# Making the second part of the first chunk's in-place sum four gate steps earlier, and part of another sum one step earlier

## The chip, the cores and the metric

The kernel runs on one core of one Trainium2 chip. The metric is the device time of one execution in microseconds (us). "PE" is TensorE (matmuls), "PEld" its weight loads, "DVE" VectorE, "ACT" ScalarE, "POOL" GpSimd, "SP" the engine that issues most transfers.

## The reference, cut to what matters

```python
xn = _layernorm(x)                               # x: 2048 rows of 448
s  = attention(xn @ wq, k_cache, v_cache) @ wo   # 16 heads of 256, window of 512 keys
g  = silu((gelu(xn @ w_gate) * (xn @ w_up)) @ w_down)    # F = 1792
return x + s * g
```

Only `g` for the first 512 rows (the first *chunk*) concerns the change. The kernel takes the rows in four chunks of 512, and F in 14 tiles of 128.

## The kernel before

The kernel keeps its own list of operations and of buffers. An operation that writes a buffer waits for the buffer's last writer and readers, and one that reads it waits for its writer:

```python
    def op(self, eng, fn, reads=(), writes=(), dma=False, after=()):
        o = Op(eng, fn, dma)
        raw = {b.writer: None for b in reads if b.writer is not None}
        deps = dict(raw)
        for b in writes:
            if b.writer is not None:
                deps[b.writer] = None
            deps.update((x, None) for x in b.readers)
        ...
```

A gate step makes two tiles of `gelu(gate) * up`. ACT applies the gelu, DVE multiplies and writes the tile `actTh` (512 columns, one buffer `b_actT[chunk][tile]`):

```python
        def gu_evac(n, b):
            c, f = divmod(n, NF)
            s = n % NGL
            act(gl[:, s, :], bank[b], ACT.Gelu_apprx_tanh, (b_ps[b],), (b_gl[s],))
            K.op("dve", lambda e: e.tensor_tensor(actTh[:, c % 2, f, :], bank[b + 1], gl[:, s, :], ALU.mult),
                 (b_ps[b + 1], b_gl[s]), (b_actT[c % 2][f],))
```

The down projection of a chunk uses seven products in place of eight (a Strassen-like scheme). For that, DVE first forms four sums of activation halves (`k` = 0 to 3), each in two parts (`i` = 0: four tiles, `i` = 1: three tiles). Sum `k = 0` goes *in place*: left half minus right half of tiles 0 to 6, written over the right half.

```python
        dn[0][0][3] = (actTh[:, 0, 0:NH, HC:QC], b_actT[0][0:NH])
        ...
            j, (x, bx), (y, by), op = ((3, o(0, 0), o(0, 1), ALU.subtract), (2, o(1, 1), S(3), ALU.subtract),
                                       (0, S(2), o(0, 0), ALU.add), (1, o(1, 0), S(2), ALU.subtract))[k]
            add("dve", S(j)[0], x, y, bx + by, S(j)[1], op)
        ...
        def down7(c, banks, g, b_g, order=(3, 6, 5, 4, 2, 1), then=None):
            ...
            product(0, B1, A(0, 0))              # "product one": left halves of tiles 0 to 6
            ...
            what = {3: (B4, A(1, 1)), 6: (B7, S(3)), 5: (B6, S(2)), 4: (B5, S(0)), 2: (B3, S(1)), 1: (B1, A(1, 0))}
            for j in order:                      # "product two" to "product seven"
                product(j, *what[j], j != 1)
```

The loop over gate steps queues these sums, from lists of (step, sum). `n` is even, and tiles `n` and `n + 1` are made in one step; the first chunk is `n` = 0 to 13, the second 14 to 27. The first chunk's down projection follows step 26.

```python
        for n in range(4, NU, 2):
            gu_group((n, n + 1), cur)
            gu_evac(n, cur[0])
            ...
            while WD_SUMS and n >= WD_SUMS[0][0]:
                sum_wd(*WD_SUMS.pop(0)[1])
            while ACT_SUMS and n >= ACT_SUMS[0][0]:
                sum_act(*ACT_SUMS.pop(0)[1])
            ...
            if n + 1 in DOWN_AT:
                ...
                end = down7(DOWN_AT[n + 1], ...)
```

The softmax here doesn't subtract the row's maximum and nothing guards it: scores larger than these inputs give would overflow.

## Time and profile before

| what | value |
|---|---|
| median, first three runs | 542.15 us |
| span of the profiled execution (541.71 us) | 539.9 us |
| PE busy | 532.9 us, 99% |
| DVE busy | 383.8 us, 71% |
| waits of PE for a sum of activations | one, 0.6 us, ending at 50.62 us |

How to read it: `bank` is a tile that matmuls write, and an *evacuation* is the operation that reads a bank out into another tile. `wdh` and `wdt` are the down weights, cast to 16 bits, and sums of them; `sd` holds the sums `k` = 1 to 3. In the attention, `kT` is keys, `va` values, `pn` softmax weights and `pT` their transpose. The prediction below shows the lines of the page, of the waits of PE, of the chain that ended last and of the timelines of PE and DVE around 50 us. In a timeline line the columns are start, length, engine, source line, operation, output and inputs, shape and count. A bracket gives the idle time before and what ended it.

### The profile page before, as it was taken

The page shows a single profiled execution, that of the slowest core. Times are in us where ns is not written, and L with a number is a line of the kernel's source. Part 1 is how long each engine was busy: PE and PEld are TensorE (multiplying, and loading weights), DVE is VectorE, ACT ScalarE, POOL GpSimd, SP SyncE. Part 2 cuts the span into 40 slices and gives each one's busy share as a digit, 9 for nine tenths or more (in the row PEclk, how much of TensorE's full clock was granted, in tenths as well). Part 3 has the DMA queues.
Part 4 walks back from the last instruction along what each step waited for, and adds up shares of the span by engine and source line. Part 5 has one row for each costly group of instructions (what it writes and reads, how often), then busy time and mean ns, then how long its engine had stood idle before and what let it go on. Part 6 is the DMA issues. An engine that isn't in the chain of part 4 may idle for free.

```text
span 539.9 us, 10920 instructions
## 1 busy us (share of the span) xinstructions
PE 532.9 (99%) x4155; PEld 310.9 (58%) x4180; DVE 383.8 (71%) x839; ACT 314.0 (58%) x782; POOL 40.1 (7%) x78
## 2 busy tenths in 40 slices
PE   9999999999999999999999999999999999999998
PEld 5556657449644444984444469544444984444487
DVE  6689785799767757935875786366667934776785
ACT  5466354873668768116866850488488106876820
POOL 1131120000000010003001000120000003001010
PEclk9999999999999999999999999999999999999999
DMA  9569172942596776302861860067448302772821
GB/s 295 125 186 108 55 124 76 263 101 46 114 186 137 154 186 153 60 1 83 167 141 50 152 137 1 18 156 140 95 106 147 70 1 69 164 158 73 148 66 35
DMA packets 171604, 61.38 MB, mean 114 GB/s; under 512 B 155104, under 2 KB 168416, under 8 KB 171552
## 3 DMA queue, kind: packets, MB, share of 16 engines
q1 hardware_dynamic: 167488, 51.30, 44.5%
q0 software_dynamic: 3008, 8.72, 6.7%
q8 instruction: 33, 0.54, 0.4%
q10 hardware_dynamic: 1056, 0.66, 0.4%
q14 instruction: 19, 0.16, 0.1%
HBM read 19.76 MB, written 3.67 MB: 43 GB/s over the span
## 4 chain that ended last, share of the span: by engine, by line
PE 92%; DVE 2%; ACT 2%; DMA 2%; issue 1%; ACTq 0%
PE bank L394 91%; ACT p L830 2%; DMA pT<-pn 2%; DVE pn L837 1%; PE bank L511 1%; DVE actTh L560 0%; DVE rden L834 0%; DVE wdt L388 0%; PE bank L492 0%; ACT gl L385 0%; DVE actTh L388 0%; DVE sd L388 0%; ACT oTh L385 0%; DVE xnT L884 0%; DVE gl L424 0%
## 5 line engine op out<-in xcount | busy, mean ns | idle before, releaser
L830 ACT ACTIVATE p<-bank 128x512 f32<-128x512 f32 x256 | 150.4, 596 | 28.1 <-DVE pn L837 25.9
L394 PE MATMUL bank<-pT,va 128*128 128x512 bf16 x512 | 120.8, 379 | 0.3
L394 PE MATMUL bank<-kT,qT 128*128 128x512 bf16 x487 | 117.8, 379 | 2.3 <-ACT qT L385 1.0
L837 DVE TENSOR_SCALAR pn<-p,rden 128x512 bf16<-128x512 f32 x256 | 113.0, 484 | 9.1 <-DMA pT<-pn 4.8
L394 PE MATMUL bank<-xnT,wq 64*128 64x512 bf16 x768 | 94.9, 376 | 0.0
L394 PEld LDWEIGHTS bank<-pT,va 128*128 128x128 bf16 x512 | 49.6, 98 | 61.3 <-DMA pT<-pn 2.3
L394 PEld LDWEIGHTS bank<-kT,qT 128*128 128x128 bf16 x512 | 49.3, 98 | 61.7 <-issue 3.4
L394 PE MATMUL bank<-xnT,wgu 64*128 64x512 bf16 (+2 forms) x768 | 84.0, 350 | 0.1
L385 ACT ACTIVATE qT<-bank 128x512 bf16<-128x512 f32 x76 | 44.1, 596 | 51.6 <-PE bank L394 49.9
L815 DVE CAST qT<-bank 128x512 bf16<-128x512 f32 x52 | 34.8, 690 | 49.3 <-PE bank L394 49.3
L394 PEld LDWEIGHTS bank<-xnT,wq 64*128 64x128 bf16 x768 | 36.7, 94 | 46.3 <-ACT p L830 1.7
L394 PEld LDWEIGHTS bank<-xnT,wgu 64*128 64x128 bf16 x768 | 37.7, 94 | 35.8 <-issue 0.6
L834 DVE RECIPROCAL rden<-rsum 128x2 f32<-128x2 f32 x128 | 21.2, 166 | 46.7 <-ACT p L830 46.5
L830 ACT ACTIVATION_READ_ACCUMULATOR p<-bank 128x1 f32 x256 | 51.6, 201 | 0.0
L394 PE MATMUL bank<-wt,sr 128*128 128x224 f16 x512 | 50.0, 259 | 0.0
L394 PEld LDWEIGHTS bank<-wt,sr 128*128 128x128 f16 x512 | 49.0, 98 | 0.4 <-ACT oTh L385 0.2
L385 ACT ACTIVATE gl<-bank 128x512 bf16<-128x512 f32 x56 | 33.0, 596 | 26.4 <-PE bank L394 22.1
L560 DVE TENSOR_TENSOR actTh<-bank,gl 128x512 f16<-128x512 f32 x56 | 37.4, 688 | 11.9 <-PE bank L394 6.4
L855 DVE TENSOR_SCALAR oTh<-bank 128x512 f16<-128x512 f32 x62 | 42.4, 684 | 0.0
L385 ACT ACTIVATE oTh<-bank 128x512 f16<-128x512 f32 x66 | 38.9, 589 | 3.9 <-PE bank L394 3.9
L394 PE MATMUL bank<-wt,oTh 128*128 128x224 f16 (+1 forms) x416 | 38.4, 252 | 0.0
L394 PEld LDWEIGHTS bank<-wt,oTh 128*128 128x128 f16 x416 | 37.2, 98 | 0.9
(77 smaller groups left out, 387.9 us busy)
## 6 DMA issues: line engine op xcount, KB each, us to landing
wtb<-in_A_wo_dram POOLq DMA_DIRECT2D x4, 896.0 KB, 10.5
wq<-in_A_wq_dram SPq DMA_DIRECT2D x2, 1536.0 KB, 8.5
va<-in_A_v_cache_dram SPq DMA_DIRECT2D x8, 256.0 KB, 6.2
pT<-pn SPq DMA_TRANSPOSE x128, 2.8
xr<-in_A_x_dram POOLq DMA_DIRECT2D x15, 112.0 KB, 2.3
wd<-in_B_w_down_dram SPq DMA_DIRECT2D x1, 1568.0 KB, 8.0
g<-g_all POOLq DMA_DIRECT2D x14, 112.0 KB, 2.3
out_dram<-xr POOLq DMA_DIRECT2D x12, 112.0 KB, 2.1
```

The source lines that it names most:

```text
L385: K.op("act", lambda e, o=o, i=i: e.activation(o, i, func, scale=scale), reads, writes)
L394: ins = e.matmul(o, lhsT=l, rhs=r, start=st, stop=sp, skip_group_check=True)
L511: ins = e.matmul(bank[b][:, 0:w], lhsT=gl[:, 0, 0:P], rhs=gl[:, 0, 0:w], start=True, stop=True)
L560: K.op("dve", lambda e: e.tensor_tensor(actTh[:, c % 2, f, :], bank[b + 1], gl[:, s, :], ALU.mult), (b_ps[b + 1], b_gl[s]), (b_actT[c % 2] ...
L815: K.op("dve", lambda v, s=s, b=b: v.tensor_copy(qT[:, s, 1, :], bank[b + 1]), (b_ps[b + 1],), (b_qT[s][1],))
L830: K.op("act", lambda e, b=b, r=r, z=z: e.activation(p32[:, z, :], bank[b], ACT.Exp, scale=att_scale, accum_out=rsum[:, r:r + 1]), (b_ps[b] ...
L834: K.op("dve", lambda e, r=r: e.reciprocal(rden[:, r - 1:r + 1], rsum[:, r - 1:r + 1]), b_rsum[r - 1:r + 1], b_rden[r - 1:r + 1])
L837: K.op("dve", lambda e, r=r - 1 + t, z=(n - 1 + t) % NP32, y=y, t=t: e.tensor_scalar(pn[:, y, t, :], p32[:, z, :], rden[:, r:r + 1], None, ...
L855: K.op("dve", lambda v, i=i, b=b: v.tensor_scalar(oTh[:, i, :], bank[b], WS, None, op0=ALU.mult), (b_ps[b],), (b_oT[i],))
```

## The change

The intent is to take the second part of the in-place sum away from the end of the second chunk's gate steps, where it stands just ahead of the down projection, and to make it at step `n = 16`. Counted in pairs of tiles from 0 over both chunks that is pair number 8, thus the second pair of the second chunk. Before, the sum was queued for 23, reached at `n = 24`.

```diff
-        ACT_SUMS = [(n, (c, k, i)) for c, i, ns in ((0, 0, (10, 11, 19, 21)), (0, 1, (23, 23, 25, 25)),
+        ACT_SUMS = sorted([(n, (c, k, i)) for c, i, ns in ((0, 0, (10, 10, 20, 22)), (0, 1, (16, 24, 26, 26)),
                                                     (1, 0, (30, 32, 34, 34)), (1, 1, (36, 36, 38, 38)))
-                    for k, n in enumerate(ns)]
+                    for k, n in enumerate(ns)], key=lambda x: x[0])
```

Since `n` is even, 11 means 12, 19 means 20, and so on. Two sums therefore move: the in-place sum's second part from 24 to 16, and the first part of the second sum (`k = 1`, tiles 7 to 10) from 12 to 10. The sorting is needed because the list is popped from its front.

## The prediction

> **What bounds the kernel now.** I began with the page. Its first part and the shares of its chain say that TensorE sets the time almost everywhere:
>
> ```profile
> PE 532.9 (99%) x4155; PEld 310.9 (58%) x4180; DVE 383.8 (71%) x839; ACT 314.0 (58%) x782; POOL 40.1 (7%) x78
> ...
> PE 92%; DVE 2%; ACT 2%; DMA 2%; issue 1%; ACTq 0%
> ```
>
> PE is counted busy for 532.9 of 539.9 us, and 92% of the chain that ended last is PE work. So the changed sums, which are VectorE work, count only where PE waits for VectorE. The waits of PE over the whole span are four lines:
>
> ```profile
> PE bank L511 <- DVE epst L425: 1.2, 1, 1.2
> PE bank L394 <- ACT qT L385: 1.0, 6, 0.2
> PE bank L394 <- DVE actTh L388: 0.6, 1, 0.6
> PE bank L394 <- issue: 0.5, 3, 0.2
> ```
>
> The third is one wait of 0.6 us for a sum over the activations (L388 is the helper for all such sums). The chain in order of time shows where: it is PE from 9.76 to about 44 us, leaves PE through VectorE, and returns at 50.62 us:
>
> ```profile
> 47.93 1.28 DVE actTh L560 x2
> 49.21 0.88 DVE wdt L388
> 50.09 0.48 DVE actTh L388
> 50.57 0.05 issue
> 50.62 67.62 PE bank L394 x644
> ```
>
> The last VectorE piece ahead of PE's return is the in-place sum, 50.09 to 50.57 us. The timeline of PE there is:
>
> ```profile
> 48.52 1.48 PE L394 MATMUL bank<-xnT,wgu 64*128 64x512 bf16 x12
> 50.62 1.52 PE L394 MATMUL bank<-wdh,actTh 128*128 128x224 f16 x14 [0.63 <-DVE actTh L388]
> 51.97 2.85 PE L394 MATMUL bank<-wdt,actTh 128*128 128x224 f16 x28
> ```
>
> That is the end of the second chunk's gate matmuls and the start of the first chunk's down projection (seven products of 14 matmuls). Its first product reads the left halves of the first chunk's activations. The in-place sum writes the right halves of the same tiles, and the kernel tracks a tile as one buffer, so the product waits for a sum whose result it doesn't read. The down projection of the second chunk has the same shape and no such wait, and gives the undisturbed rhythm:
>
> ```profile
> 76.96 1.46 PE L394 MATMUL bank<-xnT,wgu 64*128 64x512 bf16 x12
> 78.35 1.52 PE L394 MATMUL bank<-wdh,actTh 128*128 128x224 f16 x14
> 79.71 2.85 PE L394 MATMUL bank<-wdt,actTh 128*128 128x224 f16 x28
> ```
>
> **What the Trainium skill says.** "Perfetto Trace Analysis", section Tensor Engine Instruction, says that a matmul's recorded end is estimated and not observed. So I measure the stall from start to start, not by the 0.63 us idle that the timeline prints: undisturbed, product one starts 78.35 - 76.96 = 1.39 us after the last 12 gate matmuls start; here it takes 50.62 - 48.52 = 2.10 us. The stall is 0.71 us. The trace agrees with the page in that recorded matmuls overlap their successors (76.96 + 1.46 is after 78.35). "TensorE: Matmul & The Clock Gate", Part 3, section The mechanism, says matmuls start and end in strict program order; so product two can't slip past a blocked product one. The trace agrees: product two starts 1.35 us after product one, though its own operand was finished at 50.09. "VectorE: DVE Perf Modes", section Side-by-side (where the cycles go), gives 16-bit two-source operations two elements a cycle at 0.96 GHz, 0.52 ns an element. This trace agrees: the sums of 768 elements last 0.55 us and those of 1792 last 1.09 us, so 0.54 us / 1024 = 0.53 ns an element and about 0.15 us fixed. A move therefore changes no sum's duration by itself.
>
> **The change part by part.** The sums are issued after the gate steps, which run in twos. Comparing the instruction orders of the two kernels, PE, ACT, POOL and SP keep theirs; on VectorE two instructions move, and none is added or dropped.
>
> *Moved one:* the in-place sum over tiles 4 to 6 of the first chunk (768 elements, 0.55 us) goes from 50.01 us, behind the last sum over the down weights, to behind the statistics at 37.34 us. In the timeline of VectorE, with the idle before and its releaser in brackets:
>
> ```profile
> 36.69 0.62 DVE L441 BATCH_NORM_STATS2 stats<-x 128x6 f32<-128x448 bf16 x1
> 37.34 0.18 DVE L444 BATCH_NORM_AGGREGATE mv<-stats 128x2 f32<-128x6 f32 x1
> 37.99 0.69 DVE L560 TENSOR_TENSOR actTh<-bank,gl 128x512 f16<-128x512 f32 x1 [0.47 <-PE bank L394]
> ```
>
> VectorE sits idle there for 37.99 - (37.34 + 0.18) = 0.47 us. A sum that follows such an aggregate starts 0.10 us after the aggregate's start (the one at 30.93, after 30.83), so this one runs from about 37.44 to 37.99, and back-to-back records overlap by 0.08 us (52.27 + 0.55 against 52.74). The evacuation at 37.99 is then late by 0 to 0.05 us, and 0.31 us of idle at 38.99, a wait for POOL, absorbs more. Cost at its new place: 0.
>
> *Moved two:* the second sum over tiles 7 to 10 (1024 elements, 0.66 us) goes forward one step, from 30.93 us to the end of the first in-place sum at 27.54 + 0.68 = 28.22. The idle there is 0.71 us, up to 28.93, so it fits with 0.05 us to spare at most. PE uses those banks again only about 3 us after this; cost 0, gain 0.
>
> *What PE gains:* product one no longer waits for that sum. In the changed kernel its wait is on ACT (a cast of down weights, over at 44.54 + 1.74 = 46.28 us, and the last reader of its bank, over by 47.66), so nothing holds it at 48.52 + 1.39 = 49.91 us. Gain 50.62 - 49.91 = 0.71 us. The VectorE wait moves to product two, which needs the last weight sum. That ends at 50.09 as before, and product two starts at 49.91 + 1.35 = 51.26, so 1.17 us in hand. Product four needs the second sum over tiles 11 to 13, which slides forward to about 50.01 and ends at 50.57; PE reaches it at 54.66 - 0.71 = 53.95. Product five is reached at 55.3, and the sums left after the two evacuations end about 0.5 us earlier than the 53.29 of before. Nothing new binds.
>
> *Sum:* PE is 0.71 us earlier from 50 us on. The rest to the end is started by PE or bound by it, so the shift should be carried through: 542.15 - 0.71 = 541.44, rounded to 541.45. Busy time of VectorE stays at 383.8 us.
>
> **The rivals.** *A: the wait is replaced.* Product two would wait for the weight sum instead, and part of 0.71 us come back. For it: VectorE is nearly unbroken from 43.16 to 53.2 us (10.01 us busy of 10.04), and the chain runs through it. Against: the 1.17 us in hand, since product one itself takes 1.35 us. If VectorE were late by 1.5 us, the gain would shrink to 0.4 us: 541.8. *B: the gain is given back later.* The chain leaves PE again between 371 and 419 us for the softmax (activation p, pn and the transposes to pT). For it: a fixed-time arrival there would swallow the 0.7 us and give 542.1. Against: these chains start from PE's own scores, so they shift with it, and none of PE's four waits is for a DMA; PEld's waits for pT total 2.3 us in five places, so small realignments of a few tenths are possible either way. *C: the new places hurt.* If the sum at 37.4 us pushed an evacuation so far that PE waited for a bank in a later gate step, the loss could be some tenths: 541.8 to 542.3. Against: 0.47 and 0.71 us of idle under sums that take 0.55 and 0.66, and VectorE's wait for PE and POOL resets the lateness before the backlog begins. *D: more than the stall.* VectorE is earlier by 0.5 us through the epilogue of the down projection, but PE has no other wait there, so nothing adds to 0.71; only run spread could give 540.9.
>
> **Range and chances.** The centre is 541.45. The three runs of before span 542.05 to 542.58, 0.5 us, nearly the size of the effect. Allowing 0.4 us below (favourable realignment) and 0.5 us above (part of A, B or C, or spread) gives 541.0 to 542.0. The expected change is 0.71 / 542.15 = 0.13%, far inside 2%, which would take 10.8 us: within 2% 0.99, faster 0.005, slower 0.005.
>
> **What would show each step right or wrong.** Right: the waits of PE lose their line for actTh at L388; product one starts 1.39 us after the start of the last 12 gate matmuls, near 49.9 us, with product two 1.35 us later; the chain stays on PE through 44 to 50 us; the moved sums stand at about 37.4 and 28.3 us, with the idle after them gone; total VectorE busy is unchanged. Wrong: a wait of PE for wdt (A), a PE wait for an evacuation at L560 near 41 to 49 us (C), or starts that are 0.7 us earlier at 60 us but not at 400 us (B). A time at or above 542.1, outside run spread, would make the prediction wrong, and so would one below 540.9.

## The result, and the profile after

The changed kernel took 541.78 us (median of 6 runs, 541.28 to 541.98), beside 542.21 us for the kernel before (6 runs, 541.93 to 542.61). The ratio is 0.9989, with a 95% interval of 0.9977 to 1.0002. All ratios here are not quite the ratio of the medians, nor always that of the plain means. The time is inside the predicted range.

The timeline of PE in the profile after, at the same place as in the prediction's lines:

```profile
48.51 1.48 PE L394 MATMUL bank<-xnT,wgu 64*128 64x512 bf16 x12
49.91 1.51 PE L394 MATMUL bank<-wdh,actTh 128*128 128x224 f16 x14
51.27 2.85 PE L394 MATMUL bank<-wdt,actTh 128*128 128x224 f16 x28
```

Product one starts at 49.91 us, 1.40 us after the last 12 gate matmuls, and has no idle bracket any more. Before, it was 50.62 us. Product two starts 1.36 us later, without a wait. The chain of the profile after, in order of time (start, length, what), no longer leaves PE between 44 and 50 us:

```profile
9.75 107.78 PE bank L394 x1056
117.53 0.18 issue
117.72 11.07 PE bank L394 x105
```

The timeline of DVE shows where the two sums went:

```profile
28.24 0.69 DVE L388 TENSOR_TENSOR sd<-actTh 128x1024 f16<-128x1024 f16 x1
28.92 1.34 DVE L560 TENSOR_TENSOR actTh<-bank,gl 128x512 f16<-128x512 f32 x2
...
37.33 0.18 DVE L444 BATCH_NORM_AGGREGATE mv<-stats 128x2 f32<-128x6 f32 x1
37.43 0.52 DVE L388 TENSOR_TENSOR actTh<-actTh 128x768 f16<-128x768 f16 x1
37.98 0.69 DVE L560 TENSOR_TENSOR actTh<-bank,gl 128x512 f16<-128x512 f32 x1
38.99 0.61 DVE L467 TENSOR_SCALAR xn<-x,mv,rstd 128x448 bf16<-128x448 bf16 x2 [0.32 <-POOL rstd L453]
```

Both fill what was idle, and the operations after them start when they did before (28.92 against 28.93, 37.98 against 37.99, 38.99 against 38.99). But the waits of PE over the whole span also hold something new. Columns: total us, times, longest.

```profile
PE bank L511 <- DVE epst L425: 1.2, 1, 1.2
PE bank L394 <- ACT qT L385: 1.0, 6, 0.2
PE bank L394 <- issue: 0.5, 3, 0.2
PE bank L394 <- DMA pT<-pn: 0.5, 2, 0.3
PE bank L394 <- DMA va<-in_A_v_cache_dram: 0.2, 1, 0.2
```

The wait for `actTh` at L388 is gone. In its place stand waits for transfers, none of which the profile before had among its waits of PE. The timeline of PE in the profile after has them here:

```profile
172.76 1.89 PE L394 MATMUL bank<-kT,qT 128*128 128x512 bf16 x8
174.97 1.90 PE L394 MATMUL bank<-pT,va 128*128 128x512 bf16 x8 [0.32 <-DMA pT<-pn]
...
196.56 1.67 PE L394 MATMUL bank<-kT,qT 128*128 128x512 bf16 x7 [0.16 <-issue]
198.42 1.90 PE L394 MATMUL bank<-pT,va 128*128 128x512 bf16 x8 [0.19 <-DMA va<-in_A_v_cache_dram]
```

Measured from start to start, the first costs 174.97 - 172.76 = 2.21 us where 1.73 us is the rhythm (before: 175.20 - 173.47), so about 0.48 us. The second costs 1.86 us where 1.51 us is the rhythm (before: 198.29 - 196.78), so 0.35 us. At 60 us this trace is 0.71 us ahead of the one before (59.41 against 60.12). At 251 us it is 0.15 us behind (251.41 against 251.26), and its span is 540.2 us against 539.9. Yet the six runs of the changed kernel are faster on average. So the experiments had two questions. Is the freed stall the whole effect? And are these late transfers a consequence of the change, or chance?

### The profile page after: what moved, and what is told of

Read it like the earlier page. It is cut to its first block, busy times and chain, and to the rows that moved or that the text cites. A ratio compares the mean times of both kernels' runs of the same rounds, so it can differ in the third digit from the quotient of the medians.

```text
span 540.2 us, 10920 instructions
## 1 busy us (share of the span) xinstructions
PE 533.2 (99%) x4155; PEld 310.6 (58%) x4180; DVE 383.6 (71%) x839; ACT 314.2 (58%) x782; POOL 39.7 (7%) x78
## 4 chain that ended last, share of the span: by engine, by line
PE 87%; ACT 4%; DMA 4%; DVE 3%; issue 1%; SPq 1%; ACTq 0%; DVEq 0%
PE bank L394 86%; ACT p L830 4%; DMA pT<-pn 2%; DVE pn L837 2%; DMA va<-in_A_v_cache_dram 1%; PE bank L511 1%; DVE rden L834 1%; SPq L382 1%; PE bank L492 0%; DVE oTh L855 0%; ACT oTh L385 0%; DVE xnT L884 0%; DVE gl L424 0%; DVE xnT L388 0%; DVE epst L425 0%
```

## The experiments

All gave correct results. "Stall" below means the time from the start of the last 12 gate matmuls to the start of product one, less the undisturbed 1.39 us. In the kernel before it is 2.10 - 1.39 = 0.71 us.

### First job: the two moved sums apart, another cure, and the opposite dose

Before took 542.18 us here (9 runs, 541.79 to 543.5).

**e1: the in-place sum alone moved.** Relative to the changed kernel:

```diff
-(0, 0, (10, 10, 20, 22)), (0, 1, (16, 24, 26, 26))
+(0, 0, (10, 12, 20, 22)), (0, 1, (16, 24, 26, 26))
```

> Only the in-place sum is moved; the second sum stays one step later, as before. Theory (the wait of product one on the in-place sum is the whole effect): product one starts 1.39 us after the start of the last 12 gate matmuls (about 49.9 us), PE is 0.71 us earlier at 60 us than in the kernel before, and the time lies 0.4 to 0.7 us below it, as for the full change. Rival (the second sum does the work): product one still starts near 50.6 us and the time is that of before, within 0.2 us.

Measured: 541.44 us (5 runs, 541.03 to 542.89), ratio 0.9991 (0.9977 to 1.0005). The timeline of PE:

```profile
48.51 1.48 PE L394 MATMUL bank<-xnT,wgu 64*128 64x512 bf16 x12
49.92 1.52 PE L394 MATMUL bank<-wdh,actTh 128*128 128x224 f16 x14
```

The stall is gone (1.41 us), and PE is at 59.42 us where before was at 60.12. Its trace also lost time to transfers into pT, 1.0 us of PE waits in three places.

**e2: the second sum alone moved.**

```diff
-(0, 0, (10, 10, 20, 22)), (0, 1, (16, 24, 26, 26))
+(0, 0, (10, 10, 20, 22)), (0, 1, (24, 24, 26, 26))
```

> Only the second sum over tiles 7 to 10 is moved one step earlier; the in-place sum stays where it was. Theory: the stall of 0.71 us stays (product one 2.10 us after the start of the last 12 gate matmuls), and the time is that of the kernel before within 0.2 us. Rival (the second sum does part of the work): the stall is shorter than 0.6 us and the time lower by 0.2 us or more.

Measured: 541.89 us (5 runs, 541.62 to 542.72), ratio 0.9999 (0.9986 to 1.0011). The timeline of PE:

```profile
48.58 1.48 PE L394 MATMUL bank<-xnT,wgu 64*128 64x512 bf16 x12
50.68 1.51 PE L394 MATMUL bank<-wdh,actTh 128*128 128x224 f16 x14 [0.63 <-DVE actTh L388]
```

The stall is whole: 2.10 us from start to start. By the medians the time is 0.29 us below before, a little more than the 0.2 us that the text allows, but the interval of the ratio is 0.7 us wide to either side. So the times can't settle it; the stall does, and it shows no effect of the second sum.

**e3: no sum moved, but the right halves tracked on their own.** The kernel before, with the order of instructions on each engine unchanged, so that product one's wait falls away:

```diff
-        b_actT = [sbuf_bufs(a + i * NF * QC * 2, QC * 2, NF) for i in range(2)]
+        b_actT = [sbuf_bufs(a + i * NF * QC * 2, QC * 2, NF) for i in range(2)]; b_right = [K.buf() for f in range(NF // 2)]
...
-        dn[0][0][3] = (actTh[:, 0, 0:NH, HC:QC], b_actT[0][0:NH])
+        dn[0][0][3] = (actTh[:, 0, 0:NH, HC:QC], b_right)
...
-                 (b_ps[b + 1], b_gl[s]), (b_actT[c % 2][f],))
+                 (b_ps[b + 1], b_gl[s]), [b_actT[c % 2][f]] + (b_right[f:f + 1] if c % 2 == 0 and f < NH else []))
```

> The kernel before, with every instruction in its old order, but the right halves of the first chunk's tiles tracked as buffers of their own, so that product one no longer waits for the in-place sum, which it doesn't read. Theory (a wait for a whole tile where half is read): the stall goes without moving any sum, product one starts near 49.9 us, product three, which reads the sum, is reached at 52.6 us and does not wait for it (ready at 50.6); time as with the full change, 0.4 to 0.7 us below before. Rival (what counts is the backlog of VectorE, which is as before here): a wait of PE of 0.5 us or more comes back at product one or three, and the time is that of before.

Measured: 541.18 us (5 runs, 540.73 to 541.53), ratio 0.998 (0.9968 to 0.9993). The timelines of PE, then of DVE:

```profile
48.43 1.48 PE L394 MATMUL bank<-xnT,wgu 64*128 64x512 bf16 x12
49.84 1.51 PE L394 MATMUL bank<-wdh,actTh 128*128 128x224 f16 x14
```

```profile
49.04 0.96 DVE L388 TENSOR_TENSOR wdt<-wdh,wdt 128x1568 f16<-128x1568 f16 x1
49.93 0.55 DVE L388 TENSOR_TENSOR actTh<-actTh 128x768 f16<-128x768 f16 x1
```

This is the clearest run. The in-place sum runs at its old place, from 49.93 to 50.48 us. Product one starts at 49.84 us, before that sum has even begun. So product one's data never needed it: the wait was an artefact of tracking a tile as one buffer. Product three, which reads the sum, does not wait. The time lies 1.0 us below before, more than the 0.4 to 0.7 us expected; the runs e6 and e11 ask whether that was chance.

**e4: the opposite dose.**

```diff
-(0, 0, (10, 10, 20, 22)), (0, 1, (16, 24, 26, 26))
+(0, 0, (10, 12, 20, 22)), (0, 1, (26, 26, 26, 26))
```

> The opposite dose: the in-place sum is made after the two evacuations of the last gate step, about 1.2 to 1.3 us later than in the kernel before. Theory (each us by which that sum ends later is a us of PE, carried to the end): product one starts near 51.85 us, 3.3 us after the start of the last 12 gate matmuls, so PE is 1.2 to 1.3 us later at 62 us than before, and the time is 1.0 to 1.4 us above before. Rival (later slack takes up delays of this size): PE is 1.2 us late at 62 us but less than 0.6 us late by 540 us, and the time is within 0.6 us of before.

Measured: 543.92 us (5 runs, 543.18 to 544.75), ratio 1.003 (1.0016 to 1.0043), so slower beyond the noise. The edit delays a second sum too (`k` = 1, tiles 11 to 13, from 24 to 26); it starts at 52.44 us, after the in-place sum, and PE does not wait for it. The timeline of PE, then that of DVE:

```profile
48.98 1.48 PE L394 MATMUL bank<-xnT,wgu 64*128 64x512 bf16 x12
52.46 1.51 PE L394 MATMUL bank<-wdh,actTh 128*128 128x224 f16 x14 [2.01 <-DVE actTh L388]
```

```profile
49.60 0.96 DVE L388 TENSOR_TENSOR wdt<-wdh,wdt 128x1568 f16<-128x1568 f16 x1
50.60 1.34 DVE L560 TENSOR_TENSOR actTh<-bank,gl 128x512 f16<-128x512 f32 x2
51.86 0.55 DVE L388 TENSOR_TENSOR actTh<-actTh 128x768 f16<-128x768 f16 x1
```

The stall is 52.46 - 48.98 - 1.39 = 2.09 us, so 1.38 us more than before (a little over the 1.2 to 1.3 expected: the two evacuations start 1.00 us after the weight sum's start and not 0.88). Product one starts 0.05 us after the in-place sum's recorded end at 52.41. This whole execution was also 0.46 us late before it got there. The ratio, times 542.2 us, is 1.6 us with an interval of 0.9 to 2.3, so it holds the 1.38 us; the medians differ by 1.74 us, above the 1.0 to 1.4 us expected. The rival, that later slack would swallow such a delay, is refuted: the span is 543.0 us against 539.9.

### Second job: repeats, and the V load earlier

Before took 542.04 us here (11 runs, 541.37 to 544.48).

**e5: the changed kernel again,** without an edit.

> The changed kernel once more, unaltered, for a second trace and five more times. What is asked: the first trace gained 0.71 us at 50 us, then lost 0.49 us at 175 us to a late transpose into pT and 0.36 us at 198 us to the load of the sixth V head, and ended level with the kernel before. If these late transfers are chance, this trace shows the 0.71 us at 60 us again but not both losses of these sizes at the same places, and the median lies 0.4 to 0.9 us below before. If the earlier PE meets them by rule, both losses of 0.3 us or more are there again and the median is within 0.4 us of before.

Measured: 541.55 us (6 runs, 540.86 to 542.59), ratio 0.9988 (0.9971 to 1.0004). The stall is gone (1.40 us). The transpose at 175 us did not cost PE anything this time. The load of va did, 198.28 - 196.09 = 2.19 us from start to start against 1.73 us, so 0.46 us. In the timeline of PEld:

```profile
198.28 1.41 PEld L394 LDWEIGHTS bank<-pT,va 128*128 128x128 bf16 x8 [0.78 <-DMA va<-in_A_v_cache_dram]
```

So one of the two losses recurred and the other did not. The median is 0.49 us below before, as expected of chance, but this run alone leaves the va wait undecided.

**e6: the half-tracked kernel of e3 again.**

> The kernel with the right halves tracked separately once more, unaltered, on the same chip as the changed kernel. It frees the same 0.71 us. If its gain of 1.0 us against 0.4 to 0.7 us for the moved sum was chance in the transfers, the two medians of this job differ by less than 0.4 us and both lie 0.4 to 1.0 us below before. If it is better by its own nature, it is 0.4 us or more below the changed kernel again.

Measured: 541.37 us (6 runs, 540.87 to 541.69), ratio 0.9982 (0.9966 to 0.9997). It lies 0.18 us below e5, inside the 0.4 us that the text allows for chance.

**e7 and e8: the sixth V head ahead of two K transposes,** in the changed kernel (e7) and in the half-tracked one (e8):

```diff
+                        load_v(5)
                         for g in range(6, Hkv):
                             load_k(g)
-                        for g in range(5, Hkv):
+                        for g in range(6, Hkv):
                             load_v(g)
```

> The changed kernel with the load of the sixth V head queued ahead of the two K transposes of the same place and not after them, so about 2.6 us earlier. If the loss at 198 us is the queue's doing, the wait of the weight load for va at 198 us is gone, and the median is 0.1 to 0.4 us below the changed kernel of the same job. If the K transpose then comes late, a wait of PE for kT shows near 196 us and the time is the same or worse.

> Separate right halves and the sixth V head first, together, on the old order of the sums: the best version that the reasons so far can build. Theory: no wait of PE for a sum at 50 us and no wait for va at 198 us; median 0.7 to 1.1 us below before and no worse than either of its parts. If the transfers are chance and the V load seldom late, it equals the half-tracked kernel within 0.3 us.

Measured: e7 541.39 us (6 runs, 541.12 to 542.43), ratio 0.9986 (0.997 to 1.0002); e8 541.36 us (6 runs, 540.96 to 541.73), ratio 0.9983 (0.9966 to 1.0). In both traces the wait for va is gone, and no wait for kT takes its place. But e7 is only 0.16 us below e5, and e8 equals e6, so neither kernel can be told apart from the cure it is built on. For e8 the missing wait shows nothing: none of the three traces of the half-tracked kernel has a wait for va. In the changed kernel all three traces have one at the weight loads (0.7, 0.8 and 0.3 us, PEld), and so does e1 (0.2 us). e4, with the sum late, has 0.6 us, and e9, with both cures, has none. So the moved sum may have a part in it; one trace of e7 does not settle that. In the changed kernel PE itself lost 0.35, 0.46 and 0 us to it.

### Third job: is separate tracking better, or was that chance?

After two jobs the half-tracked kernel looked 0.4 us better than the changed one, and both its traces were free of the losses that both traces of the changed kernel had. The last four runs test that. Before took 542.41 us here (11 runs, 541.62 to 544.27).

**e9: both cures at once,** the edit of e3 in the changed kernel.

> The changed kernel (sums moved) with the right halves tracked separately as well. The 0.71 us can be freed only once, so product one starts 1.39 us after the last 12 gate matmuls and no earlier. Theory (the two cures remove the same wait and the rest of any difference is chance in late transfers): the mean lies 0.4 to 1.0 us below before and within 0.4 us of both cures of this job. Rival (the moved sums cost about 0.4 us somewhere that separate halves do not): it is like the changed kernel, and 0.3 us or more above the half-tracked kernel.

Measured: 542.03 us (6 runs, 541.3 to 542.58), ratio 0.999 (0.9975 to 1.0004). The stall is gone, and no more than that (1.41 us from start to start). The mean is 0.58 us below before, as the theory had it, and its trace loses time to transfers like those of the changed kernel (PE waits of 0.80 us at 264 us and 0.65 us at 420 us).

**e10: the changed kernel a third time.**

> The changed kernel a third time. Over its first two jobs its mean was 0.57 and 0.65 us below before. Theory: 0.4 to 1.0 us below before; from 160 to 490 us this trace takes 0 to 1 us longer than the shortest such trace, 331.6 us, with the losses at PE waits for transposes into pT or for va. Rival (the change itself costs 0.9 us in that stretch): again 332.4 us or more, as in both its traces so far.

Measured: 541.73 us (6 runs, 541.14 to 542.71), ratio 0.9983 (0.9967 to 0.9998). The traced execution, the slowest of the six, lost time at a place where neither earlier trace of this kernel had, and had no wait of PE for va (only 0.3 us of its weight loads):

```profile
263.90 0.82 PE L394 MATMUL bank<-pT,va 128*128 128x512 bf16 x3 [1.24 <-DMA pT<-pn]
```

**e11: the half-tracked kernel a third time.**

> The half-tracked kernel a third time, beside the changed one. Over its first two jobs its mean was 1.22 and 0.96 us below before. Theory (same 0.71 us, the rest chance): 0.4 to 1.0 us below before and within 0.4 us of the changed kernel. Rival (better by its own nature): 0.4 us or more below the changed kernel again, with 331.8 us or less from 160 to 490 us as in both traces so far.

Measured: 542.15 us (6 runs, 541.03 to 543.8), ratio 0.9996 (0.9977 to 1.0014). The advantage did not repeat, and both figures of the theory were missed: by the means it lies 0.27 us below before and 0.50 us above the changed kernel of the same job. Its traced execution, the fastest of its six, again had 331.6 us from 160 to 490 us, but three of its others took 542.74 to 543.8 us.

**e12: the kernel before, traced a second time.**

> The kernel before, unaltered, for a second trace of it and as a measure of chance. Its first trace happened to be from a fast execution, with no loss to transfers between 160 and 490 us (331.6 us). Expected: product one 2.10 us after the last 12 gate matmuls again; a ratio to before of 1.000 within 0.001; and 331.6 to 332.6 us from 160 to 490 us, so that losses of some tenths to transfers occur without any change.

Measured: 542.53 us (6 runs, 541.79 to 543.54), ratio 1.0003 (0.9987 to 1.0018). The timeline and the waits of PE:

```profile
48.51 1.47 PE L394 MATMUL bank<-xnT,wgu 64*128 64x512 bf16 x12
50.61 1.52 PE L394 MATMUL bank<-wdh,actTh 128*128 128x224 f16 x14 [0.62 <-DVE actTh L388]
```

```profile
PE bank L394 <- DMA pT<-pn: 0.6, 2, 0.4
PE bank L394 <- DVE actTh L388: 0.6, 1, 0.6
```

The stall is the same to 0.01 us. The unchanged kernel too loses time to transfers into pT; its first trace just happened to show none. The one near 419 us (0.28 us here) stands in 12 of the 14 traces, with and without the stall.

The lines for `ACT qT` and `issue` of the first trace are missing here. They stand, the same each time, in the six traces with 4155 records of PE (the first ones of the two kernels and e1 to e4), and in none of the eight with 4180; of 512 score matmuls the first trace of before has 487 on record. Before each such 0.16 us a group has one matmul fewer (x7 at 196.78 us before, x8 at 196.75 us in e12). So they are lost records and not waits: of the prediction's four lines of waits, two were real. The differences above compare groups with the same count.

### What the twelve say together

The table gives, for each trace, the stall and the length of the attention part: from the start of the first score matmuls after 159 us to the start of those near 491 us, both read from the timeline of PE (for before: 491.43 - 159.87).

| kernel | stall, us | attention part, us | ratio to before |
|---|---|---|---|
| before, first trace | 0.71 | 331.56 | – |
| before, e12 | 0.71 | 332.22 | 1.0003 |
| second sum alone, e2 | 0.71 | 332.62 | 0.9999 |
| in-place sum late, e4 | 2.09 | 332.68 | 1.003 |
| changed, first | 0.01 | 332.55 | 0.9989 |
| changed, e5 | 0.01 | 332.44 | 0.9988 |
| changed, e10 | 0.01 | 333.11 | 0.9983 |
| in-place sum alone, e1 | 0.02 | 332.45 | 0.9991 |
| half-tracked, e3 | 0.02 | 331.73 | 0.998 |
| half-tracked, e6 | 0.02 | 331.66 | 0.9982 |
| half-tracked, e11 | 0.02 | 331.63 | 0.9996 |
| both cures, e9 | 0.02 | 332.97 | 0.999 |
| changed, V first, e7 | 0.01 | 331.68 | 0.9986 |
| half-tracked, V first, e8 | 0.02 | 331.71 | 0.9983 |

The stall is the same to 0.01 us in every trace of a kind, and every kernel without it has a ratio below 1. The mean of the changed kernel's three ratios is 0.9987, and 0.0013 of 542.2 us is 0.7 us: the freed 0.71 us. For the half-tracked kernel the mean of three is 0.9986. By the plain means of the runs the changed kernel lies 0.58, 0.65 and 0.77 us below before in its three jobs, 0.67 on average. On the other hand the attention part varies by 1.5 us between traces, with PE waits at 175, 198, 264, 362, 379 and 419 us. It varies in kernels that have the stall (by 1.1 us over four traces) and in those that don't (by 1.5 us over ten), and the two groups have nearly the same mean, 332.27 and 332.19 us.

The traces also show that the stall is carried to the end. Take for each trace how much later than in the first one the last 12 gate matmuls start, and add the difference in the stall and the difference in the attention part. The sum gives the span of every trace to 0.15 us: for the changed kernel's first trace, -0.01 - 0.70 + 0.99 = 0.28 us, and its span is 0.3 us longer. In the five traces without the stall whose attention part is as short as in the first trace (e3, e6, e7, e8, e11), the span is 539.2 or 539.3 us against 539.9.

By the letter of e10's text the rival's figure (332.4 us or more) came out for the changed kernel three times, and the theory's (at most 332.6 us) was missed by e10. I don't take that as a cost of the change, though it is not excluded by traces: all five traces with the in-place sum moved earlier and the V load in its old place have 332.4 us or more. The largest loss was at a different place each time (175, 198 and 264 us). The traced executions of the changed kernel were the slowest, the second slowest and the slowest of their six. Its fastest run of all, 540.86 us, is 0.51 us below the fastest of before (541.37 us), which speaks against a built-in loss of 0.9 us. And its three jobs average the full 0.7 us. A difference of some tenths between the two cures can't be excluded with these runs: the half-tracked kernel was 0.31 us faster in the second job and 0.50 us slower in the third. No version is shown to beat the changed kernel.

## Why the prediction was right

**The stall and its cause** were right. The prediction said that product one waits for a sum whose result it doesn't read; e3 shows it directly, since there product one starts before that sum begins.

**The size, 0.71 us from start to start,** was right: 2.10 - 1.40 = 0.70 us freed in each of the three traces of the changed kernel. Reading 0.63 us from the idle bracket would have been 0.08 us short.

**The costs of the new places** were right at zero. The prediction had the second sum end within 0.05 us of the next evacuation and the in-place sum run from 37.44 to 37.99; the trace has evacuations that start no later than before, and a sum from 37.43 to 37.95. That a move changes no sum's duration was nearly so: the second sum took 0.69 us and not 0.66, ending 0.01 us past the next start on record, and the in-place sum 0.52 us and not 0.55. Rival C is out.

**The margin of product two** was right (rival A is out). Product two starts at 51.27 us, 0.01 us from the figure on record, and the weight sum ends at 50.09 (49.13 + 0.96). The remaining sums finish 0.60 us earlier than before (52.69 against 53.29), not about 0.5; nothing hangs on it. DVE busy is 383.6 against 383.8 us.

**The carrying to the end** was right on the average of three jobs, and hidden by scatter in any single one. The first result's median gain of 0.43 us, and its ratio's 0.0011 x 542.2 = 0.6 us, fall short of 0.71 by less than the runs scatter. That the time fell into the range says little by itself: the range ends 0.15 us below the time before. By the prediction's own sign for rival B the first trace even shows B: PE is 0.71 us ahead at 60 us and 0.21 us behind near 400 us (399.72 against 399.51). The other traces show that this came from late transfers in that execution: the unchanged kernel has such losses too, and where they are small the gain reaches the end. The weak sentence in the prediction is the one against rival B, "none of PE's four waits is for a DMA". It was true of the trace, but that trace was of an execution of 541.71 us, faster than each of the six runs of before in the first result. The second trace of the same kernel has 0.6 us of such waits. The prediction did allow "small realignments of a few tenths"; they measure up to 1.5 us between traces.

What stays open is why a transpose into pT, or the V load, is late in one execution and not in another. No run here shows what the transfers met.

## What to carry to other kernels

Where the busiest engine waits, ask whether it needs the data at all: half a tile tracked as a whole tile cost 0.71 us here, and could be cured by moving the writer into idle time or by finer tracking alike. Measure a stall from start to start, against an undisturbed copy of the same passage. And when a predicted gain is as small as the scatter of runs, check the mechanism in the trace at the place of the change, and repeat jobs before reading anything into what happens hundreds of microseconds later.

## What the Trainium skill lacked or had wrong

- "Perfetto Trace Analysis", section Tensor Engine Instruction, was right that a matmul's end is estimated. It does not say what that does to the size of a gap: here the bracket shows 0.63 us idle for a stall of 0.71 us.
- I found no page with the scatter of the landing of a transpose, from issue on. Transposes into pT take 2.7 us at the least, 2.7 or 2.8 at the median and 4.7 to 5.4 at the most in the traces here, and PE stands idle for up to 1.24 us for one.
